# Seven products for two tiles of the last key group, and gated rows read back two steps later

## The chip, the cores and the metric

The kernel runs on one core of one Trainium2 chip. The metric is the device time of one execution in microseconds. Before the change it is 2479.84 us, the median of three runs (2478.89 to 2482.92).

## What is computed

An attention block without softmax is followed by a mixture of experts whose routing is a hash of the token number. Cut to what matters:

```python
# B, S, D, K = 8, 2496, 256, 64;  E, F = 8, 1024;  float32 throughout
scores = (1 / S) * z @ z.transpose(0, 2, 1)      # symmetric, S x S in each batch
x = u * (np.maximum(scores, 0) ** 2 @ v)         # B x S x D
x = x.reshape(B * S, D)
expert = token_ids * 2654435761 % E
for e in range(E):
    out[expert == e] = np.maximum(x[expert == e] @ w1[e], 0) @ w2[e]
```

## The kernel before

**Tiles and groups.** The 2496 tokens of a batch are 20 tiles of 128, the last of 64 rows. Four tiles make a group; groups are numbered g = 0 to 4, and batches b = 0 to 7. For each batch and each group of queries the kernel runs over the five groups of keys. Scores are symmetric, so a block of scores is computed once, with keys on the partitions; where the mirrored block is needed, it is turned by 32x32 transposes on VectorE. Some mirrors are turned in place of the tile, others go through one of three buffers named `stage` (L300) and are carried by DMAs of SyncE, `m<-stage` (L307). The attention phase fills about the first 1452 us, the MoE phase the rest.

**Key groups and their order.** `units` lists the groups of keys in the order in which a group of queries takes them. Its own group (the diagonal) comes last; the group of the last keys, k = 4, comes right before it when g is 1, 2 or 3. `mixed` says which key groups are computed by seven products of half-size blocks in place of eight (Winograd's form of Strassen's scheme): `product` issues one of them, and the table `PRODUCTS` gives the order, `[(1, 6), (5, 7), (2, 3), (4,)]`. A key group that is not mixed is taken tile by tile by `attend`, with two products of 512 columns for each tile, one for each half of the features; the last keys are one of these: three whole tiles, and the 64-row tile in `attend_last` at the start of the diagonal. All accumulate in four banks of PSUM, `acc`.

**Half-sums.** Four of the seven products need sums and differences of blocks of scores. `mix_a` makes them on GpSimd: three operations, L430 (two sums in one), L431 and L432, into one of two buffers `a_mix` (named `as`); a buffer comes free when its key group's products are done. `mix_a` is called at the start of each key group and ahead of the diagonal. Sums of the values, `v_mix` (named `vs`), are made on VectorE by `mix_v`.

**From the banks to the rows.** `post` (L462 to L468) adds the banks into `o_way`; `gate` (L475) transposes that into `x_q` on VectorE and puts three later steps on a list. After step i + 1, four DMAs of SyncE write the rows to DRAM (`x_way<-x_q`, L487). After step i + 3, SyncE reads them back as rows of tokens (`x_sb<-x_way`, L496). Five steps after that, `rows_by_u` copies the token numbers to the side of the rows on VectorE (L506) and multiplies the four tiles by u on GpSimd (L509). Then one tile after each step is scattered to `x_rows`, sorted by expert, with an indirect DMA on GpSimd (`place_x`, L749). One buffer `x_sb` and one `x_q` serve all groups.

**What sets the order.** The whole attention phase is written out by hand, in `tc.manual_schedule()`: after each step of products comes some work of ScalarE (squares of scores), some transposes, and `between`, which runs the steps of the list that are due and one scatter. Instructions of one engine run in the order in which they are issued here, and so do the DMAs of one queue.

Of the kernel before, what the change touches and what calls it, by code (L numbers as in the profile page):

```python
# [10 lines left out]
F32 = mybir.dt.float32  # L11
# [13 lines left out]
def kernel(  # L25
# [10 lines left out]
    nc = tc.nc  # L36
# [63 lines left out]
    zero = const.tile([P, W], F32)  # L100
    nc.gpsimd.memset(zero[:, 0:D], 0.0)
    nc.gpsimd.memset(zero[:, D:W].bitcast(I32), N)
    ident = const.tile([P, P], F32)
    make_identity(nc, ident[:])

# [2 lines left out]

    def group(g):
        return range(g * G, min(T, g * G + G))

    def tiles_io(dram, b, tiles, sb, store, eng, twice=False):

# [41 lines left out]
                    nc.scalar.dma_start(o[:, t], m)  # L157

    v_free = [vpool.tile([P, G, D], F32, name=f"v_{k}") for k in range(NG + 1)]
    v_mix = [vpool.tile([P, 4, G // 2, P], F32, name=f"vs_{k}") for k in range(NG - 1)]  # L160
    a_mix = [vpool.tile([P, 4, G * P], F32, name=f"as_{k}") for k in range(2)]
    o_way = vpool.tile([P, 4 * G * P // 2], F32, name="o_way")

    def load_v(b, g):
        v_sb[b, g] = v_free.pop(0)
# [4 lines left out]
    def mix_v(b, g):  # L170

        v = v_sb[b, g]
        (a11, a21), (a12, a22) = ([v[:, ts(k, G // 2), c::2] for c in range(2)] for k in range(2))
        s1, s2, s3, s4 = (v_mix[g][:, k] for k in range(4))
        nc.vector.tensor_add(s1, a21, a22)
        nc.vector.tensor_sub(s2, s1, a11)
        nc.vector.tensor_sub(s3, a11, a21)
        nc.vector.tensor_sub(s4, a12, s2)
# [5 lines left out]
    def turn_z(b, g):  # L184
        if g == 0:
            zT[b] = zpool.tile([P, T * P], F32, name="zT")
        if b:
            nc.vector.transpose(zT[b][:, ts(g, G * P)], zn[b][:, ts(g, G)].rearrange("p t j k -> p (t j k)"))
            return


        pairs = group(g) if g < NG else [T]
        ps = mm_ps.tile([P, G * P], F32, name="z_ps", tag="mm")
        for i, t in enumerate(pairs):
            nc.tensor.transpose(ps[:, ts(i, P)], zn[b][:, t:t + 2].rearrange("p t k -> p (t k)"), ident[:])
        i = 0 if g else 1
        n = len(pairs)
        copies = [nc.scalar.copy(zT[b][0:K, ds((g * G + i - 1) * P, (n - i) * P)], ps[0:K, i * P:n * P])]
        if g < NG:
            copies.append(nc.vector.tensor_copy(zT[b][K:P, ts(g, G * P)], ps[K:P, :]))  # L200

        for c, own, other in zip(copies, ("upper", "lower"), ("lower", "upper")):
            tc.declare_no_dep(c.ins, group=other, reason="other rows of zT")
            tc.add_to_no_dep_group(own, c.ins)
# [29 lines left out]

    def mixed(b, g, k):

        return k < NG - 1 and (b > 0 or g > 2)

    def skipped(b, g, t):

# [167 lines left out]
    def blocks(b, g, k):  # L408

        n = queries(g) // Q  # L410
        if k >= g:
            x = made[b, k, g] if k < g else made[b, g, k]
            return x[:].rearrange("p (k s) (h q) -> p k h s q", k=2, h=2)
        x = mirror[b, k, g][:].rearrange("p i r s q -> p (i r) (s q)")[:, 0:n]
        return x.rearrange("p (h n) (k y) -> p k h n y", h=2, k=2)

    def mix_a(most=2):

        for e in to_mix[:min(most, 2 - len(a_made))]:
            b, g, k = e  # L420
            turn_now((b, k, g))
            while any(x[0:2] == (b, g) and x[2] // G == k for x in to_square):
                square(1)
            tile = a_free.pop(0)
            n = queries(g)
            x = blocks(b, g, k)
            y = x.shape[3:]
            sums = [tile[:, m, 0:n].rearrange("p (n y) -> p n y", n=y[0]) for m in range(4)]
            t13 = tile[:, 0:2, 0:n].rearrange("p m (n y) -> p m n y", n=y[0])
            nc.gpsimd.tensor_sub(t13, x[:, :, 1], x[:, 0])  # L430
            nc.gpsimd.tensor_sub(sums[2], x[:, 1, 1], sums[0])  # L431
            nc.gpsimd.tensor_sub(sums[3], x[:, 1, 0], sums[2])  # L432
            a_made[e] = tile, sums
            to_mix.remove(e)

    def product(b, g, k, m):

        v, vs = v_sb[b, k], v_mix[k]
        n = queries(g) // Q // 2
        sums = a_made[b, g, k][1]  # L440
        for s in range(G // 2):
            if m in (1, 2, 4):
                w = v[:, s + (0 if m == 1 else 2), (1 if m == 4 else 0)::2]
            else:
                w = vs[:, {5: 0, 6: 1, 7: 2, 3: 3}[m], s]
            if m in (1, 2, 3):
                t = k * G + s + (0 if m == 1 else 2)
                x = squares(b, g, t)[:, ts(1 if m == 3 else 0, n)]
            else:
                x = sums[{5: 0, 7: 1, 6: 2, 4: 3}[m]]  # L450
                x = x[:, s].rearrange("p (n q) -> p n q", q=Q) if k >= g else x[:, :, ts(s, Q)]
            times((0, 1, 2, 3)[{1: 0, 6: 0, 5: 1, 7: 1, 2: 2, 3: 2, 4: 3}[m]], n * Q if m in (6, 7, 3) else 0, w, x)
# [17 lines left out]
    def gate(b, g, h):  # L470
        n = queries(g) // Q
        if h == 0:
            x_q[b, g] = qpool.tile([P, G * NQ, D // NQ], F32, name="x_q")
        x = x_q[b, g]
        nc.vector.transpose(x[:, 0:n, h::2], (o_way[:, ts(h, n * Q)] if any(mixed(b, g, k) for k in range(NG)) else acc[2 + h][:, 0:n * Q])  # L475
                            .rearrange("p (n q) -> p n q", q=Q))
        if h == 0:
            return

        xs = xpool.tile([P, G, W], F32, name="x_sb")  # L480
        o = x_way[groups.index((b, g)) % len(x_way)]

        ends = (b, g) == groups[-1]
        queues = [nc.sync, nc.scalar if ends else nc.sync]
        def rows_away():
            for a in range(NQ):
                queues[a % 2].dma_start(o[:].rearrange("n p d -> p n d")[:, 0:n, ts(a, D // NQ)], x[ts(a, Q), 0:n])  # L487
        if ends:
            rows_away()
        else:  # L490
            to_fetch.append((i + 1, rows_away))
        m = len(whole(g))
        def rows_of_x():

            w = o[:].rearrange("(i r) p d -> (r p) i d", r=NQ)
            queues[0].dma_start(xs[:, 0:m, 0:D], w[:, 0:m])  # L496
            if m < G:
                queues[0].dma_start(xs[0:R, m, 0:D], w[0:R, m])
            if (b, g) == groups[0]:
                load_u(b, g)  # L500
            to_fetch.append((i + 5, rows_by_u))
        def rows_by_u():
            for lo, n, rows in ((0, m, P), (m, len(group(g)) - m, R)):
                if n:
                    whose = token[0:rows, b, ds(g * G + lo, n)]
                    nc.vector.tensor_copy(xs[0:rows, lo:lo + n, D:W].bitcast(I32), whose.unsqueeze(2).to_broadcast([rows, n, W - D]))  # L506
            for k, t in enumerate(group(g)):
                y = xs[0:width(t), k, 0:D]
                (nc.vector if ends else nc.gpsimd).tensor_mul(y, y, u_sb[b, g][0:width(t), k, :])  # L509
                gated.append((b * T + t, xs[0:width(t), k, :]))  # L510
            if (b, g) == groups[-2]:
                while gated:
                    place_x()
            if not ends:
                to_fetch.append((i + 3, lambda: load_u(*groups[groups.index((b, g)) + 1])))
        to_fetch.append((max(i + 3, SORT + 2 + 14 * groups.index((b, g))), rows_of_x))

# [6 lines left out]
    extra = const.tile([1, 1], I32)  # L526
    slot_i = const.tile([P, C], I32)
    token = const.tile([P, B, T], I32)

    tok = const.tile([P, B, T, 2], I32)  # L530

    def clear_x(k):
        c = NW * BLK // P + k * -(-NT // CLEAR)
# [320 lines left out]
    for n, (b, g) in enumerate(groups):  # L854
# [10 lines left out]
        steps = []  # L865
        for x, k in enumerate(seq):
            last = k == g
            if mixed(b, g, k):
                banks = (0, 1, 2, 3) if x == 0 and g or last else (2, 1, 0, 3)
                part = [(lambda k=k, m=m: [product(b, g, k, e) for e in PRODUCTS[m]], m, 1 if m < 3 else 0.5) for m in banks]  # L870
            elif last:
                part = [(lambda t=[t for t in group(k) if t < TM], h=h: [attend(b, g, e, [h]) for e in t], 2 + h, 1.5)
                        for h in range(2)]
            else:
                part = [(lambda t=t: attend(b, g, t, range(2)), None, 1) for t in group(k) if t < TM]
            steps.append(part)
        t = 0
        for x, k in enumerate(seq):
# [18 lines left out]
            for y, (step, bank, weight) in enumerate(steps[x]):  # L897
                if k != g:
# [22 lines left out]
                            attend_last(b, g)  # L921
                    if b + 1 < B and (g, t) == (1, 9):
                        load_v(b + 1, NG - 1)
                    if (b, g) == (0, 2) and t in (4, 7, 10, 13):
                        mix_v(0, t // 3 - 1)
                if k == g and not ends and d:
                    scores(c, d, y * G, (y + 1) * G if y + 1 < len(steps[x]) else T)
                step()
# [483 lines left out]
```

## Time and profile before

| | before |
|---|---|
| median of three runs | 2479.84 us |
| the profiled execution | 2480.39 us |
| its span, first to last instruction | 2478.2 us |
| mean granted clock of TensorE | 0.996 |
| TensorE busy | 2448.0 us, 99% |
| VectorE busy | 1650.5 us, 67% |
| ScalarE busy | 740.5 us, 30% |
| GpSimd busy | 1322.2 us, 53% |

An engine's busy share is an average over both phases. In the page's names PE is the matmul unit, PEld its weight loads, DVE is VectorE, ACT ScalarE, POOL GpSimd, SP SyncE. The profile records each float32 matmul as two matmuls and two weight loads. In the rows of a timeline, instructions that follow each other without a gap and are alike stand as one row, with their count after an x.

### The profile page before, as it was taken

To read this page: it belongs to the slowest core of one execution; us is meant where nothing else is said; L and a number is where in the kernel's file an instruction comes from. 1 tells how busy PE (TensorE), PEld (TensorE's weight loads), DVE (VectorE), ACT (ScalarE), POOL (GpSimd) and SP (SyncE) were. 2 spreads that over 40 slices of the span, in tenths; PEclk is the share of its full clock that TensorE was granted. 3 is DMA by queue.
4 is the path that set the end of the run, shared out by engine and by line. 5 is a ranking of instruction groups with operands and counts; after the bars stand their busy time and mean duration, and the time that the engine had idled before them with its cause. 6 is when DMAs were issued, how large, how long until landed. Compare 5 with 4: busy or idle time off the path is not lost. (4 is left out here: it accounts for less than half of the span.)

```text
span 2478.2 us, 38152 instructions
## 1 busy us (share of the span) xinstructions
PE 2448.0 (99%) x12691; PEld 1963.8 (79%) x12691; DVE 1650.5 (67%) x3556; ACT 740.5 (30%) x1532; POOL 1322.2 (53%) x1078
## 2 busy tenths in 40 slices
PE   9999999999999999999999999999999999999998
PEld 4466777777777776776777769989998998998998
DVE  5887777787787786886787725556556556556534
ACT  5222324233232233234134102332232232323222
POOL 1357876776785876776777832333333333333314
PEclk9999999999999999999999999999999999999999
DMA  4364553454454535534534379769668767777751
GB/s 122 90 143 115 137 114 107 118 129 107 112 122 111 121 106 128 112 102 124 120 107 112 89 181 229 178 171 212 175 175 201 173 170 201 188 179 177 179 137 45
DMA packets 512966, 348.06 MB, mean 140 GB/s; under 512 B 289788, under 2 KB 475645, under 8 KB 512768
## 3 DMA queue, kind: packets, MB, share of 16 engines
q1 hardware_dynamic: 410512, 254.82, 42.9%
q10 hardware_dynamic: 86800, 48.57, 8.3%
q0 software_dynamic: 15456, 42.20, 5.1%
q8 instruction: 103, 1.69, 0.3%
q14 instruction: 95, 0.78, 0.1%
HBM read 231.19 MB, written 68.19 MB: 121 GB/s over the span
## 5 line engine op out<-in xcount | busy, mean ns | idle before, releaser
L268 ACT ACTIVATE a<-s_ps 128x512 f32<-128x512 f32 (+2 forms) x470 | 216.7, 547 | 930.4 <-PE s_ps L258 852.2
L403 PE MATMUL acc<-a,v 128*128 128x512 f32 (+4 forms) x1352 | 462.0, 507 | 0.0
L403 PE MATMUL acc<-as,vs 128*128 128x256 f32 (+1 forms) x1776 | 422.0, 378 | 13.6 <-POOL as L431 9.7
L403 PEld LDWEIGHTS acc<-a,v 128*128 128x128 f32 (+1 forms) x1352 | 243.5, 196 | 183.3 <-issue 151.1
L403 PEld LDWEIGHTS acc<-as,vs 128*128 128x128 f32 x1776 | 336.8, 191 | 64.7 <-POOL as L431 13.7
L1278 POOL DMA_INDIRECT out_dram<-as,ids x120 | 123.2, 1027 | 469.4 <-DVE as L1177 441.2
L296 DVE STREAM_TRANSPOSE m<-a 32x512 f32<-32x512 f32 (+1 forms) x512 | 350.6, 685 | 8.7 <-ACT a L274 0.8
L324 DVE STREAM_TRANSPOSE a<-a 32x128 f32<-32x128 f32 (+2 forms) x1360 | 286.6, 241 | 13.2 <-ACT a L274 2.3
L274 ACT ACTIVATE a<-a 128x512 f32<-128x512 f32 (+1 forms) x480 | 238.3, 591 | 22.7 <-DMA m<-stage 22.5
L1050 PE MATMUL h_ps<-v,as 128*128 128x256 f32 x904 | 223.7, 380 | 0.0
L300 DVE STREAM_TRANSPOSE stage<-a 128x512 f32<-128x512 f32 x192 | 131.1, 696 | 127.4 <-DMA m<-stage 126.4
L258 PE MATMUL s_ps<-zT 64*128 64x512 f32 (+1 forms) x960 | 212.5, 558 | 1.3 <-ACT a L274 0.9
L430 POOL TENSOR_TENSOR as<-a 128x1024 f32<-128x1024 f32 x71 | 169.1, 2382 | 74.2 <-ACT a L274 39.7
L749 POOL DMA_INDIRECT x_rows<-x_sb,slot_i x160 | 158.2, 989 | 91.1 <-issue 28.9
L430 POOL TENSOR_TENSOR as<-m 128x1024 f32<-128x1024 f32 (+1 forms) x77 | 173.6, 2254 | 41.0 <-DMA m<-stage 29.8
L509 POOL TENSOR_TENSOR x_sb<-x_sb,u_sb 128x256 f32<-128x256 f32 (+1 forms) x156 | 109.6, 735 | 158.1 <-DMA x_sb<-x_way 135.7
L1050 PEld LDWEIGHTS h_ps<-v,as 128*128 128x128 f32 x904 | 171.9, 190 | 23.4 <-DVE v L1029 0.4
L403 PE MATMUL acc<-m,v 128*128 128x256 f32 (+2 forms) x664 | 177.2, 392 | 1.7 <-issue 1.5
L258 PEld LDWEIGHTS s_ps<-zT 64*128 64x128 f32 x960 | 98.9, 187 | 93.0 <-issue 60.3
L1066 DVE TENSOR_TENSOR hT<-stage,h_ps 128x512 f32<-128x512 f32 x111 | 76.2, 687 | 134.2 <-PE h_ps L1050 130.1
L403 PEld LDWEIGHTS acc<-m,v 128*128 128x128 f32 x664 | 126.9, 197 | 47.4 <-issue 38.6
L403 PE MATMUL acc<-as,v 128*128 128x256 f32 (+1 forms) x592 | 149.4, 375 | 0.0
(220 smaller groups left out, 3829.2 us busy)
## 6 DMA issues: line engine op xcount, KB each, us to landing
m<-in_moe_w_dram SPq DMA_DIRECT2D x200, 256.0 KB
m<-in_moe_w_dram SPq DMA_DIRECT2D x50, 1024.0 KB
m<-stage SPq DMA_DIRECT2D x576, 64.0 KB
x_way<-x_q SPq DMA_DIRECT2D x128, 128.0 KB
u_sb<-in_u_dram ACTq DMA_DIRECT2D x32, 512.0 KB
x_sb<-x_way SPq DMA_DIRECT2D x32, 512.0 KB
v<-x_rows SPq DMA_DIRECT2D x128, 128.0 KB
zn<-in_moe_w_dram SPq DMA_DIRECT2D x64, 256.0 KB
```

Of the source, the lines that this page charges most:

```text
L258: nc.tensor.matmul(ps[:, lo:n], zT[b][h, ts(t, P)], zT[b][h, ds(g * G * P + lo, n - lo)], start=True, stop=True)
L268: nc.scalar.activation(a, ps[:, lo:n], AF.Relu)
L274: nc.scalar.activation(a, a, AF.Square, scale=1.0 / S)
L296: nc.vector.transpose(o, x[ts(r, Q), 0:m * G, ts(c, Q)].rearrange("p (i s) q -> p i s q", s=G))
L300: nc.vector.transpose(stage[:].rearrange("p (n q) -> p n q", q=Q), x[:, :, ts(c, Q)])
L324: return n * Q, lambda: nc.vector.transpose(out, in_)
L403: nc.tensor.matmul(acc[k][:, ds(at, n)], weights, x, start=k not in begun, stop=True, skip_group_check=True)
L430: nc.gpsimd.tensor_sub(t13, x[:, :, 1], x[:, 0])
L509: (nc.vector if ends else nc.gpsimd).tensor_mul(y, y, u_sb[b, g][0:width(t), k, :])
L749: st = nc.gpsimd.indirect_dma_start(out=x_dram[:, :], out_offset=bass.IndirectOffsetOnAxis(ap=slot_i[0:width(c % T), c:c + 1], axis=0), in ...
L1050: nc.tensor.matmul(ps[:, ts(i, W)], terms[k][0][:, ts(2 * d + i, P)], terms[k][1], start=first and i == 0, stop=True, skip_group_check=True)
L1278: st = nc.gpsimd.indirect_dma_start(out=out[:], out_offset=bass.IndirectOffsetOnAxis(ap=rows, axis=0), in_=o, in_offset=None, bounds_check ...
```

## The change

**Which groups are mixed.** Where products are mixed at all, the last keys are now mixed for the query groups 1, 2 and 3. That holds in seven batches for three groups and in the first batch for group 3. Of the last keys' three whole tiles, tile 18 is still taken plainly, as the first step; tiles 16 and 17 are one block of two halves, one tile each, and their seven products are the second and third steps: (2, 3, 1, 6) and (5, 7, 4). `half(k)` gives the tiles in a half: 2, or 1 for the last keys. For this there is a fifth buffer of value sums and four VectorE operations per batch. To make room for it, the token table `tok` and the identity `ident` now lie in `o_way`, which they use before the first `post` writes it.

**When rows come back.** The read-back of the gated rows is put on the list for i + 5 in place of i + 3; the multiply still follows five steps after it. The copy of the token numbers moves from ahead of the multiply to ahead of the read-back.

```diff
+    def half(k):
+        return G // 2 if k < NG - 1 else 1
...
-    v_mix = [vpool.tile([P, 4, G // 2, P], F32, name=f"vs_{k}") for k in range(NG - 1)]
+    v_mix = [vpool.tile([P, 4, half(k), P], F32, name=f"vs_{k}") for k in range(NG)]
...
+    tok = o_way[:, 0:B * T * 2].bitcast(I32).rearrange("p (b t two) -> p b t two", b=B, two=2)
+    ident = o_way[:, ds(B * T * 2, P)]
+    make_identity(nc, ident)
...
     def mixed(b, g, k):
-        return k < NG - 1 and (b > 0 or g > 2)
+        return (b > 0 or g > 2) and (k < NG - 1 or 0 < g < NG - 1)
...
-            x = made[b, k, g] if k < g else made[b, g, k]
-            return x[:].rearrange("p (k s) (h q) -> p k h s q", k=2, h=2)
+            x = made[b, g, k][:, 0:2 * half(k), 0:queries(g)]
+            return x.rearrange("p (k s) (h q) -> p k h s q", k=2, h=2)
...
         def rows_of_x():
+            for lo, n, rows in ((0, m, P), (m, len(group(g)) - m, R)):
+                if n:
+                    whose = token[0:rows, b, ds(g * G + lo, n)]
+                    nc.vector.tensor_copy(xs[0:rows, lo:lo + n, D:W].bitcast(I32), whose.unsqueeze(2).to_broadcast([rows, n, W - D]))
             w = o[:].rearrange("(i r) p d -> (r p) i d", r=NQ)
             queues[0].dma_start(xs[:, 0:m, 0:D], w[:, 0:m])
...
             to_fetch.append((i + 5, rows_by_u))
         def rows_by_u():
-            for lo, n, rows in ((0, m, P), (m, len(group(g)) - m, R)):
-                if n:
-                    whose = token[0:rows, b, ds(g * G + lo, n)]
-                    nc.vector.tensor_copy(xs[0:rows, lo:lo + n, D:W].bitcast(I32), whose.unsqueeze(2).to_broadcast([rows, n, W - D]))
...
-        to_fetch.append((max(i + 3, SORT + 2 + 14 * groups.index((b, g))), rows_of_x))
+        to_fetch.append((max(i + 5, SORT + 2 + 14 * groups.index((b, g))), rows_of_x))
...
-            if mixed(b, g, k):
+            if mixed(b, g, k) and k == NG - 1 and not last:
+                part = [(lambda: attend(b, g, TM - 1, range(2)), None, 1)]
+                part.extend((lambda k=k, m=m: [product(b, g, k, e) for e in m], None, 1) for m in ((2, 3, 1, 6), (5, 7, 4)))
+            elif mixed(b, g, k):
...
-                    if (b, g) == (0, 2) and t in (4, 7, 10, 13):
-                        mix_v(0, t // 3 - 1)
+                    if (b, g) == (0, 2) and t in (1, 4, 7, 10, 13):
+                        mix_v(0, (t // 3 - 1) % NG)
+                    if b and (g, t) == (0, 9):
+                        mix_v(b, NG - 1)
```

GpSimd in a second group (g = 1) of a later batch, from the fourth key group's half-sums to the diagonal's; `as` is a half-sum buffer, `a` a block of scores, L430 to L432 and after them L436 to L438 are the three operations of `mix_a`. Before:

```order
L430 TENSOR_TENSOR as_107<-a 128x1024
L431 TENSOR_TENSOR as_107<-a,as_107 128x512
L432 TENSOR_TENSOR as_107<-a,as_107 128x512
L509 TENSOR_TENSOR x_sb<-x_sb,u_sb 128x256 x4
L749 DMA x_rows<-x_sb,slot_i 20480x272 x2
L430 TENSOR_TENSOR as_108<-a 128x1024
L431 TENSOR_TENSOR as_108<-a,as_108 128x512
L432 TENSOR_TENSOR as_108<-a,as_108 128x512
L749 DMA x_rows<-x_sb,slot_i 20480x272 x2
```

And now:

```order
L436 TENSOR_TENSOR as_104<-a 128x1024
L437 TENSOR_TENSOR as_104<-a,as_104 128x512
L438 TENSOR_TENSOR as_104<-a,as_104 128x512
L436 TENSOR_TENSOR as_103<-a 128x2x256
L437 TENSOR_TENSOR as_103<-a,as_103 128x256
L438 TENSOR_TENSOR as_103<-a,as_103 128x256
L515 TENSOR_TENSOR x_sb<-x_sb,u_sb 128x256 x4
L753 DMA x_rows<-x_sb,slot_i 20480x272 x4
L436 TENSOR_TENSOR as_104<-a 128x1024
L437 TENSOR_TENSOR as_104<-a,as_104 128x512
L438 TENSOR_TENSOR as_104<-a,as_104 128x512
```

The last keys' half-sums stand between the fourth key group's and the multiply, and the diagonal's half-sums stand behind four scatters in place of two.

TensorE at the end of the same group, the last keys and the start of the diagonal; `v` are values, `vs` their sums, `s_ps` scores of the next group. Before:

```order
L403 MATMUL acc<-a,v_101 128x512 x8
L258 MATMUL s_ps<-zT 128x512 x4
L403 MATMUL acc<-a,v_98 128x256 x2
L403 MATMUL acc<-as_108,vs_104 128x256 x2
L258 MATMUL s_ps<-zT 128x512 x4
```

And now:

```order
L409 MATMUL acc<-a,v_96 128x512 x2
L409 MATMUL acc<-a,v_96 128x256
L409 MATMUL acc<-a,vs_102 128x256
L409 MATMUL acc<-a,v_96 128x256
L409 MATMUL acc<-as_104,vs_102 128x256 x3
L409 MATMUL acc<-as_104,v_96 128x256
L409 MATMUL acc<-a,v_96 128x512 x2
L264 MATMUL s_ps<-zT 128x512 x4
L409 MATMUL acc<-a,v_93 128x256 x2
L409 MATMUL acc<-as_103,vs_99 128x256 x2
```

Four of the eight products of 512 columns (six of three whole tiles, two of the 64-row tile) became seven of 256, and four of those read half-sums of GpSimd.

VectorE in the first group (g = 0) of a later batch, around the copy of the token numbers of the group before; `stage` are carried mirrors, `m` mirrors turned in place. Before:

```order
L296 STREAM_TRANSPOSE m_192<-a 32x4x128
L300 STREAM_TRANSPOSE stage<-a 128x512 x4
L506 COPY x_sb<-token 128x4x16
L300 STREAM_TRANSPOSE stage<-a 128x512 x5
L462 COPY o_way<-acc 128x256
```

And now:

```order
L302 STREAM_TRANSPOSE m_191<-a 32x4x128 x3
L504 COPY x_sb<-token 128x4x16
L302 STREAM_TRANSPOSE m_191<-a 32x4x128
L306 STREAM_TRANSPOSE stage<-a 128x512 x3
L181 TENSOR_TENSOR vs_102<-v_97 128x128
L182 TENSOR_TENSOR vs_102<-vs_102,v_97 128x128
L183 TENSOR_TENSOR vs_102<-v_97 128x128
L184 TENSOR_TENSOR vs_102<-v_97,vs_102 128x128
L306 STREAM_TRANSPOSE stage<-a 128x512 x5
L468 COPY o_way<-acc 128x256
```

The copy stood among the transposes of the carried mirrors and now stands ahead of them; the four sums of the last keys' values have come in among them.

## Rows read from the trace of the kernel before

**Rows 1.** The page, section 1: busy time of each engine, share, instructions.
```profile
PE 2448.0 (99%) x12691; PEld 1963.8 (79%) x12691; DVE 1650.5 (67%) x3556; ACT 740.5 (30%) x1532; POOL 1322.2 (53%) x1078
```
**Rows 2.** TensorE's waits: line waited for, us in total, times, longest us.
```profile
PE acc L403 <- POOL as L431: 9.7, 10, 4.9
```
**Rows 3.** Timeline, TensorE: start, us, instruction, [idle before it and what ended it].
```profile
214.55 6.18 PE L403 MATMUL acc<-a,v 128*128 128x512 f32 x16
...
619.32 1.03 PE L403 MATMUL acc<-a,v 128*128 128x256 f32 x4
620.18 1.03 PE L403 MATMUL acc<-a,vs 128*128 128x256 f32 x4
...
635.05 1.13 PE L403 MATMUL acc<-as,vs 128*128 128x256 f32 x4 [0.53 <-POOL as L431]
```
**Rows 4.** Timeline, GpSimd, first and second group of the fourth batch.
```profile
587.65 1.01 POOL L749 DMA_INDIRECT x_rows<-x_sb,slot_i  x1 [3.60 <-DVE x_sb L506]
...
592.45 2.38 POOL L430 TENSOR_TENSOR as<-a 128x1024 f32<-128x1024 f32 x1
...
626.04 2.77 POOL L509 TENSOR_TENSOR x_sb<-x_sb,u_sb 128x256 f32<-128x256 f32 x4 [7.79 <-DMA x_sb<-x_way]
628.96 1.01 POOL L749 DMA_INDIRECT x_rows<-x_sb,slot_i  x1 [0.15 <-POOL x_sb L509]
...
631.27 2.38 POOL L430 TENSOR_TENSOR as<-a 128x1024 f32<-128x1024 f32 x1
633.73 1.27 POOL L431 TENSOR_TENSOR as<-a,as 128x512 f32<-128x512 f32 x1
```
**Rows 5.** Timeline, SyncE's DMA issues, second group of the fourth batch.
```profile
585.69 29.88 SPq L307 DMA_DIRECT2D m<-stage  x44
615.68 3.30 SPq L487 DMA_DIRECT2D x_way<-x_q  x4
619.08 2.55 SPq L307 DMA_DIRECT2D m<-stage  x4
621.95 0.38 SPq L496 DMA_DIRECT2D x_sb<-x_way  x1
```
**Rows 6.** Groups by line and form: count | busy us, mean ns | idle before.
```profile
L403 PEld LDWEIGHTS acc<-as,vs 128*128 128x128 f32 x1776 | 336.8, 191 | 64.7 <-POOL as L431 13.7 <-issue 11.7 <-POOL as L430 4.6
```
**Rows 7.** Timeline, GpSimd and TensorE, diagonals of other second groups.
```profile
455.17 1.26 POOL L431 TENSOR_TENSOR as<-a,as 128x512 f32<-128x512 f32 x1
...
457.93 1.03 PE L403 MATMUL acc<-as,vs 128*128 128x256 f32 x4
...
811.67 1.13 PE L403 MATMUL acc<-as,vs 128*128 128x256 f32 x4 [0.57 <-POOL as L431]
...
1165.48 1.13 PE L403 MATMUL acc<-as,vs 128*128 128x256 f32 x4 [1.20 <-POOL as L431]
...
1343.54 1.13 PE L403 MATMUL acc<-as,vs 128*128 128x256 f32 x4 [0.97 <-POOL as L431]
```
**Rows 8.** Timeline, GpSimd and TensorE, first group of the second batch.
```profile
234.65 1.01 POOL L749 DMA_INDIRECT x_rows<-x_sb,slot_i  x1 [6.74 <-DVE x_sb L506]
...
240.70 2.07 PE L403 MATMUL acc<-as,vs 128*128 128x256 f32 x4 [4.90 <-POOL as L431]
```
**Rows 9.** Timeline, GpSimd and TensorE, end of attention, first MoE product.
```profile
1436.58 2.10 POOL L430 TENSOR_TENSOR as<-m 128x896 f32<-128x896 f32 x1
...
1438.73 3.35 PE L403 MATMUL acc<-as,vs 128*128 128x224 f32 x8 [3.45 <-POOL as L430]
...
1453.81 15.70 PE L995 MATMUL h_ps<-v,m 128*128 128x512 f32 x32 [2.52 <-DVE v L843]
```
**Rows 10.** Windows: us, then PE, PEld, DVE, ACT, POOL busy, PEclk, DMA, GB/s.
```profile
240.80:246.40 5.60, 5.60 (x12) 2.26 (x12) 1.73 (x3) 1.09 (x2) 5.13 (x4) 0.50 0.56 148
1438.80:1444.40 5.60, 5.60 (x15) 5.04 (x16) 0.00 (x0) 0.00 (x0) 2.21 (x2) 0.50 0.49 97
1454.80:1458.10 3.30, 3.30 (x5) 1.32 (x4) 0.00 (x0) 0.60 (x1) 0.00 (x0) 0.50 0.45 87
1165.50:1172.00 6.50, 6.50 (x30) 4.07 (x31) 2.58 (x5) 3.03 (x6) 5.94 (x5) 1.00 0.57 144
```

More of the change, by code (lines that the diff above doesn't have):

```diff
@@ L102 @@
     nc.gpsimd.memset(zero[:, D:W].bitcast(I32), N)
-    ident = const.tile([P, P], F32)
-    make_identity(nc, ident[:])
     def width(t):
@@ L172, in mix_v @@
         v = v_sb[b, g]
-        (a11, a21), (a12, a22) = ([v[:, ts(k, G // 2), c::2] for c in range(2)] for k in range(2))
+        (a11, a21), (a12, a22) = ([v[:, ts(k, half(g)), c::2] for c in range(2)] for k in range(2))
         s1, s2, s3, s4 = (v_mix[g][:, k] for k in range(4))
@@ L194, in turn_z @@
         for i, t in enumerate(pairs):
-            nc.tensor.transpose(ps[:, ts(i, P)], zn[b][:, t:t + 2].rearrange("p t k -> p (t k)"), ident[:])
+            nc.tensor.transpose(ps[:, ts(i, P)], zn[b][:, t:t + 2].rearrange("p t k -> p (t k)"), ident)
         i = 0 if g else 1
@@ L424, in mix_a @@
             tile = a_free.pop(0)
-            n = queries(g)
             x = blocks(b, g, k)
             y = x.shape[3:]
+            n = y[0] * y[1]
             sums = [tile[:, m, 0:n].rearrange("p (n y) -> p n y", n=y[0]) for m in range(4)]
@@ L440, in product @@
         sums = a_made[b, g, k][1]
-        for s in range(G // 2):
+        for s in range(half(k)):
             if m in (1, 2, 4):
-                w = v[:, s + (0 if m == 1 else 2), (1 if m == 4 else 0)::2]
+                w = v[:, s + (0 if m == 1 else half(k)), (1 if m == 4 else 0)::2]
             else:
@@ L446, in product @@
             if m in (1, 2, 3):
-                t = k * G + s + (0 if m == 1 else 2)
+                t = k * G + s + (0 if m == 1 else half(k))
                 x = squares(b, g, t)[:, ts(1 if m == 3 else 0, n)]
@@ L528 @@
     token = const.tile([P, B, T], I32)
-    tok = const.tile([P, B, T, 2], I32)
     def clear_x(k):
```

## The prediction

> **What bounds the kernel now.** The page's first section comes first: TensorE is busy in 2448.0 of 2478.2 us [rows 1], so the time is the length of TensorE's instructions and the few gaps between them. An edit counts if it shortens that queue, or opens or closes a gap. The list of TensorE's waits comes second: ten waits for the second half-sum of scores that GpSimd makes for a diagonal group (line 431) hold 9.7 us, the longest 4.9 [rows 2]. The reader should see in these rows that the bank products already lean on GpSimd, and with how little room. The third view shows by how little: in the second group of the fourth batch TensorE stood 0.53 us before the diagonal's first product on half-sums, at 635.05 [rows 3]. GpSimd was late since its order there is multiply by u, two scatters, diagonal mix, and the multiply, free after 7.79 us of idling, waited for the rows to come back from DRAM until 626.04; the scatters began at 628.96, the mix at 631.27, and its second part began at 633.73 and took 1.27 [rows 4]. SyncE says why the rows came then: 44 sends of mirror stages without a gap from 585.69, then the four writes of x_way, four more sends, then the read-back at 621.95 [rows 5]. That chain is paced by VectorE's transposes into three stage buffers, not by TensorE.
>
> **Columns saved.** The last keys' three whole tiles cost two products of 512 columns for each half, each recorded as two matmuls. The 16 records from 214.55 are twelve of those and four of 256 columns, 6.18 us in all; four of 256 alone are recorded with 1.03 us, so one of 512 takes (6.18 - 1.03) / 12 = 0.43 us, and as the next four follow 0.86 us later (619.32 to 620.18), one of 256 takes 0.215 [rows 3]. Two of the tiles are 8 x 0.43 = 3.44 us; seven products on their halves are 14 x 0.215 = 3.01. A saving of 0.43 us in each of 22 groups (three in seven batches, one in the first) gives **-9.4 us**, all on the path.
>
> Each of the 14 records has a weight load of its own, where there were 8. In this kernel 1776 such loads take 191 ns each [rows 6], and the records above still follow each other in 215 ns, so the loads lie beside the matmuls. The Trainium skill ("TensorE: Matmul & The Clock Gate", Part 3, "The mechanism") says that a weight load overlaps matmuls in flight only when its row group differs, and here all have all 128 rows. By that rule 14 x (0.215 + 0.19) = 5.7 us would replace 8 x (0.43 + 0.19) = 5.0, and the change would lose 0.7 x 22 = 15 us; the trace does not agree, since 256-column records of one row group stand 0.215 apart, not 0.41.
>
> **The new sums.** GpSimd makes the last keys' half-sums at half size. No row has that size; the full ones take 2.38 and 1.27 us [rows 4], and the third, of the second's size, as much, so half is 2.5 and the whole size, the upper bound, 4.9. I take 2.8, nearer the half with some start cost. They can begin when products free the second buffer (about 619.3 in the stretch above) and end at 622, within the 7.79 us idle; TensorE wants them only behind one plain tile and four records. Cost 0, and up to 2 us a group if the idle were absent. VectorE's four value sums (four operations of 128x128 a batch) go beside 67% busy VectorE: 0. Token numbers and the identity sharing the output buffer: 0, since both are read before it is written.
>
> **Scatters ahead of the diagonal's mix.** One scatter is issued each step. The read moves two steps later in the program, but SyncE issues it as soon as what stands ahead of it in its queue is through; in the second groups that queue's 44 sends and the four writes are the same, so the rows land at the same time. The multiply still waits for them and GpSimd's order becomes: last keys' sums, multiply, **four** scatters, diagonal mix. Behind the waiting multiply stand the mix and TensorE's products. Four scatters before a mix took 592.45 - 587.65 = 4.80 us, two took 631.27 - 628.96 = 2.31 [rows 4]: the mix is 2.5 later. TensorE also arrives 0.4 sooner by the columns and 0.3 sooner by the gaps of the first groups, closed below. So the margin of each second group shrinks by 3.2. Four of the six such groups waited already (0.53 [rows 3], 0.57, 1.20 and 0.97 [rows 7], 3.3 together), and each waits 3.2 more: 3.7 to 4.4. In the other two the mix was ready early: its second part ended at 455.17 + 1.26 = 456.4 where the product began at 457.93 [rows 7]; less that margin of 1.5 each waits 1.7. Together 4 x 3.2 + 2 x 1.7 = **+16.2 us**. If the rows landed earlier this goes to zero (a rival); if by two steps later, up to 3 us a group more.
>
> In the third and fourth groups the order is the same, but 12 stage sends stand ahead of the writes, where the second groups have 16 to 24, so rows return earlier than TensorE's need by an estimated 2 to 4 us. I take +3 for all of them and the two odd groups of the first two batches, between 0 and 26.
>
> **Gaps that close.** In the first group of the second batch a scatter waited 6.74 us for VectorE's token copy, which stood in a run of stage transposes, and TensorE waited 4.90 us for the mix behind it [rows 8]. With the copy issued ahead of the read that goes. The other five waits (9.7 - 4.9 - 3.3 = 1.5 us) are in first groups with the same order and go too. In the last group the mix of the fourth key group moves ahead of the multiply and scatters, so the wait of 3.45 us at 1438.73 goes; but the last eight scatters now come behind its three parts, some 4 us later (the first part alone takes 2.10), and the MoE part's first product, at 1453.81 after a gap of 2.52, waits for rows that they write [rows 9].
>
> **The clock.** After idles of 4.90, 3.45 and 2.52 us [rows 8, 9] TensorE's granted clock was 0.50 (1.2 GHz) for 5.6, 5.6 and 3.3 us of the stretches shown; after the wait of 1.20 us [rows 7] it stayed at 1.00 [rows 10]. Half the time is lost: 2.8, 2.8 and 1.65 us. So closing the first two gives 4.90 + 2.8 = **-7.7** and 3.45 + 2.8 = 6.3, of which the later start of the MoE part takes back 2 to 6: **-3.5**. The four waits of 3.7 to 4.4 us lie between 2.52 and 4.90; I price each at the mean of 1.65 and 2.8, 2.3: **+9.2**, bounds 0 and 11. The two of 1.7 us lie nearer 1.20: 0.
>
> **The sum.** -9.4 - 7.7 - 1.5 - 3.5 + 16.2 + 9.2 + 3 = +6.3 us. The profiled execution took 2480.4 (2478.2 of span and 2.2 around it), so 2486.7; the median is 0.55 lower: **2486**.
>
> **Rivals.** (a) *No new wait, the other side.* If the last sends ahead of x_way finish some 4 us sooner once VectorE's token copies leave the transposes' way, the rows land early, the existing second-group waits (3.3) vanish and no new ones come: -9.4 - 7.7 - 1.5 - 3.3 - 3.5 + 3 = -22.4, so 2457.5. It decides from a multiply that begins 3.2 us or more earlier against TensorE than 626.04. For it: GpSimd idles 7.79 us just there [rows 4]. Against it: the sends run gapless from 585.69 [rows 5] and a token copy is one short operation. (b) *The waits come, the clock stays.* Without its 9.2 us the sum is -2.9: 2477. For it: only three such idles are on record. (c) *The third and fourth groups wait as well*, 12 of them by 2 us, with the 24 in place of 2 of the 3: 2508. For it: the same order on GpSimd; against it: fewer sends ahead. (d) *Loads not hidden*, the rule above: +15 for -9.4, 2511. *That the change does not do what it says* has no room: the products replace the tiles in TensorE's order in 22 groups.
>
> **Chances.** Forecast 46% (2478 to 2495), (a) 21%, (b) 19%, (c) 11%, (d) 3%. A measurement of this kernel can tell some 0.2%, 5 us, from no change. (a) and a fifth of (b) are faster: 25%. The rest of (b) and the lowest tenth of the forecast are within: 20%. The rest is slower: 55%. The range leaves out the lower part of (a), about 9%, and the upper half of (c) with (d), 9%: 2457 to 2507. The forecast's own is 2478 to 2495.
>
> **What would show it.** Right: TensorE's waits on line 437 (431 before) gather at the diagonals of the second groups, 3.5 to 4.5 us each, with a clock of 0.50 behind them; the scatters run by fours ahead of the diagonal mix; multiplies still idle for the rows; the gaps of 4.90 and 3.45 are gone; last keys' records stand 0.215 apart. Wrong: a multiply that begins early enough, or waits that appear at the last keys' products instead, which would put the price on the new sums.

## The result and the profile after

The changed kernel takes 2509.3 us in the median (2505.2 to 2514.3, six runs) against 2480.3 before (2478.0 to 2482.9): 1.0115 times as long, with a 95% interval of 1.0105 to 1.0125. It is slower by some 29 us, as forecast in sign, but by five times the +6 of the sum, and 2 us past the upper end of the range. The profiled execution took 2513.8 us, 4.5 above the median; the sums below are made against its own span.

The page's first lines, and the list of TensorE's waits (engine, what waited, line waited for: us in total, times, longest). L436 to L438 are the three parts of `mix_a`, L468 to L474 `post`, L504 the token copy, L506 the read-back, L515 the multiply, L753 the scatter:

```profile
span 2512.1 us, 38566 instructions
PE 2457.3 (98%) x12823; PEld 1994.1 (79%) x12823; DVE 1690.7 (67%) x3588; ACT 741.8 (30%) x1532; POOL 1381.7 (55%) x1144
PE acc L409 <- POOL as L437: 26.2, 10, 4.1
PE acc L409 <- POOL as L436: 3.6, 2, 3.1
PE acc L409 <- DVE o_way L469: 3.5, 1, 3.5
PE h_ps L1059 <- DVE vs L847: 2.1, 1, 2.1
```

The 9.7 us of [rows 2] have become 26.2, again in ten waits, and TensorE is busy 9.3 us longer [rows 1] although its queue has fewer columns: the clock was at half more often, as the next table shows.

To find where the 33.9 us of span went, I cut TensorE's timeline at the start of each group's diagonal, and each piece into waits, time lost to half clock (half of every stretch at a granted clock of 0.50, as far as TensorE was not waiting in it), and the rest. Numbers in us, after minus before; a second group has g = 1, a fourth g = 3:

| where | waits | half clock | forecast |
|---|---|---|---|
| six diagonals of second groups | +15.9 | +12.4 | +16.2 and +9.2 |
| diagonals of fourth groups (four of them) | +7.1 | +1.7 | +3 with all others |
| first batch, its last group (g = 4) | +3.5 | +1.5 | 0 |
| first batch, its fourth group | -0.7 | 0 | 0 |
| second batch, first group | -0.8 | +0.1 | -7.7 |
| five other first groups | -1.6 | 0 | -1.5 |
| small new waits for `post` (first and last groups) | +2.8 | 0 | 0 |
| fourth key group's half-sums in the last group | -3.5 | -2.9 | -6.3 |
| start of the MoE part | +2.1 | +1.7 | +2.8 |
| the rest, mostly columns | -6.6 | | -9.4 |

(With 1.3 us at the program's start, which varies as much between the runs below, the waits, the half clock and the rest sum to the 33.9 within 0.1.)

The second group of the fourth batch, GpSimd and then TensorE, is what was forecast:

```profile
639.49 2.78 POOL L515 TENSOR_TENSOR x_sb<-x_sb,u_sb 128x256 f32<-128x256 f32 x4 [4.92 <-DMA x_sb<-x_way]
642.42 1.01 POOL L753 DMA_INDIRECT x_rows<-x_sb,slot_i  x1 [0.15 <-POOL x_sb L515]
...
646.31 0.98 POOL L753 DMA_INDIRECT x_rows<-x_sb,slot_i  x1 [0.30 <-issue]
647.31 2.36 POOL L436 TENSOR_TENSOR as<-a 128x1024 f32<-128x1024 f32 x1
649.74 1.26 POOL L437 TENSOR_TENSOR as<-a,as 128x512 f32<-128x512 f32 x1
...
651.06 1.13 PE L409 MATMUL acc<-as,vs 128*128 128x256 f32 x4 [3.48 <-POOL as L437]
```

From the multiply's start to the diagonal's half-sums it is 7.8 us, where it was 5.2 [rows 4]: two scatters more. GpSimd idled 4.92 us for the rows where it had idled 7.79; the last keys' half-sums fitted in there, and TensorE had no wait at the last keys. Behind this 3.48 us wait the clock was at half, and behind that of 3.85 us at 1195.54 for twice as long (columns as in [rows 10]):

```profile
652.60:655.80 3.20, 3.20 (x9) 0.96 (x6) 1.10 (x3) 1.25 (x3) 3.12 (x2) 0.50 0.12 28
1195.60:1202.00 6.40, 6.40 (x14) 2.95 (x15) 1.47 (x3) 1.72 (x4) 6.08 (x4) 0.50 0.13 29
```

In the fourth group of the third batch the read-back came later against TensorE. SyncE's queue, GpSimd and TensorE before, then the same after, with TensorE's wait:

```profile
505.21 2.40 SPq L487 DMA_DIRECT2D x_way<-x_q  x4
510.18 0.38 SPq L496 DMA_DIRECT2D x_sb<-x_way  x1
...
522.41 1.27 POOL L431 TENSOR_TENSOR as<-a,as 128x512 f32<-128x512 f32 x1
...
526.82 1.46 PE L403 MATMUL acc<-as,vs 128*128 128x256 f32 x6
```
```profile
516.30 2.49 SPq L493 DMA_DIRECT2D x_way<-x_q  x4
518.89 3.40 SPq L313 DMA_DIRECT2D m<-stage  x4
522.54 0.40 SPq L506 DMA_DIRECT2D x_sb<-x_way  x1
...
527.69 2.78 POOL L515 TENSOR_TENSOR x_sb<-x_sb,u_sb 128x256 f32<-128x256 f32 x4 [3.78 <-DMA x_sb<-x_way]
...
535.50 2.37 POOL L436 TENSOR_TENSOR as<-a 128x1024 f32<-128x1024 f32 x1
...
539.27 4.11 PE L409 MATMUL acc<-as,vs 128*128 128x256 f32 x10 [2.40 <-POOL as L437]
```

Two steps later in the program, four stage sends (3.40 us) now lie between the writes and the read-back. The read-back comes 6.2 us after the writes began, not 5.0. Before, the half-sum that the product needs was ready 3.1 us ahead of it (522.41 + 1.27 against 526.82); now it is 2.4 us late. Of these 5.5 us, 2.6 are the two scatters more between the multiply and the half-sums, and 2.9 the later multiply. From the third batch on, such new sends between writes and read-back stand in the third and the sixth batch alone; the waits in the fourth groups of the fourth and the seventh batch (0.7 and 1.1 us) come without them.

In the first two batches three things are new. VectorE stood idle at two token copies, waiting for the scatters of the group ahead:

```profile
193.94 0.50 DVE L504 COPY x_sb<-token 128x64 int32<-128x64 int32 x1 [2.36 <-DMA x_rows<-x_sb,slot_i]
277.72 0.49 DVE L504 COPY x_sb<-token 128x64 int32<-128x64 int32 x1 [3.77 <-DMA x_rows<-x_sb,slot_i]
```

After the first of these, VectorE's value sums ran while GpSimd made half-sums. TensorE waited for the banks to be added. VectorE, GpSimd, TensorE:

```profile
202.70 3.05 DVE L181 TENSOR_TENSOR vs<-v 128x256 f32<-128x256 f32 x1
205.85 1.30 DVE L182 TENSOR_TENSOR vs<-vs,v 128x256 f32<-128x256 f32 x1
207.08 1.49 DVE L183 TENSOR_TENSOR vs<-v 128x256 f32<-128x256 f32 x1
208.49 2.56 DVE L184 TENSOR_TENSOR vs<-v,vs 128x256 f32<-128x256 f32 x1
...
203.07 2.38 POOL L436 TENSOR_TENSOR as<-a 128x1024 f32<-128x1024 f32 x1
205.53 1.34 POOL L437 TENSOR_TENSOR as<-a,as 128x512 f32<-128x512 f32 x1
206.95 1.33 POOL L438 TENSOR_TENSOR as<-a,as 128x512 f32<-128x512 f32 x1
208.25 2.52 POOL L436 TENSOR_TENSOR as<-a 128x1024 f32<-128x1024 f32 x1
...
212.60 2.07 PE L409 MATMUL acc<-a,v 128*128 128x256 f32 x4 [3.52 <-DVE o_way L469]
```

Each sum ends 0.3 us after one of GpSimd's operations. And in the next group the rows of the group ahead were read back at 259.52, behind twenty sends, so the multiply and the half-sums behind it were late in place of the closed gap:

```profile
244.68 14.61 SPq L313 DMA_DIRECT2D m<-stage  x20
259.52 0.41 SPq L506 DMA_DIRECT2D x_sb<-x_way  x1
...
263.38 2.77 POOL L515 TENSOR_TENSOR x_sb<-x_sb,u_sb 128x256 f32<-128x256 f32 x4 [5.18 <-DMA x_sb<-x_way]
...
271.04 3.78 PE L409 MATMUL acc<-as,vs 128*128 128x256 f32 x8 [3.11 <-POOL as L436]
```

### The profile page after: what moved, and what is told of

Same layout as the page of the kernel before. It is cut to its first block, busy times and chain, and to the rows that moved or that the text cites. A ratio compares the mean times of both kernels' runs of the same rounds, so it can differ in the third digit from the quotient of the medians.

```text
span 2512.1 us, 38566 instructions
## 1 busy us (share of the span) xinstructions
PE 2457.3 (98%) x12823; PEld 1994.1 (79%) x12823; DVE 1690.7 (67%) x3588; ACT 741.8 (30%) x1532; POOL 1381.7 (55%) x1144
## 5 line engine op out<-in xcount | busy, mean ns | idle before, releaser
L409 PE MATMUL acc<-as,vs 128*128 128x256 f32 (+1 forms) x1908 | 459.9, 381 | 31.7 <-POOL as L437 26.2
L409 PEld LDWEIGHTS acc<-as,vs 128*128 128x128 f32 x1908 | 364.3, 193 | 90.9 <-POOL as L437 30.4
L409 PE MATMUL acc<-a,v 128*128 128x256 f32 (+4 forms) x1264 | 412.6, 488 | 3.5 <-DVE o_way L469 3.5
L409 PEld LDWEIGHTS acc<-a,v 128*128 128x128 f32 (+1 forms) x1264 | 226.8, 197 | 148.8 <-issue 109.6
L436 POOL TENSOR_TENSOR as<-a 128x1024 f32<-128x1024 f32 (+1 forms) x93 | 196.4, 2111 | 105.1 <-PE acc L409 63.0
L264 PE MATMUL s_ps<-zT 64*128 64x512 f32 (+1 forms) x960 | 218.1, 571 | 0.6 <-DVE zT L194 0.5
L753 POOL DMA_INDIRECT x_rows<-x_sb,slot_i x160 | 158.6, 991 | 74.0 <-issue 30.5
L436 POOL TENSOR_TENSOR as<-m 128x1024 f32<-128x1024 f32 (+1 forms) x77 | 173.2, 2249 | 47.4 <-DMA m<-stage 34.2
L409 PE MATMUL acc<-as,v 128*128 128x256 f32 (+1 forms) x636 | 162.9, 376 | 2.1 <-DVE o_way L474 1.5
L515 POOL TENSOR_TENSOR x_sb<-x_sb,u_sb 128x256 f32<-128x256 f32 (+1 forms) x156 | 110.9, 743 | 83.8 <-DMA x_sb<-x_way 83.5
```

The source lines that it names most:

```text
L264: nc.tensor.matmul(ps[:, lo:n], zT[b][h, ts(t, P)], zT[b][h, ds(g * G * P + lo, n - lo)], start=True, stop=True)
L409: nc.tensor.matmul(acc[k][:, ds(at, n)], weights, x, start=k not in begun, stop=True, skip_group_check=True)
L753: st = nc.gpsimd.indirect_dma_start(out=x_dram[:, :], out_offset=bass.IndirectOffsetOnAxis(ap=slot_i[0:width(c % T), c:c + 1], axis=0), in ...
```

## Experiments

Theory A: the loss is made by the place of the multiply, which waits for rows, and of the scatters in GpSimd's order. Rival B: a later read-back in SyncE's queue costs by itself. Rival C: the products cost what they save. A2 is on the first batch: the token copy holds VectorE.

**1. Read-back nine steps after the gate.**

```diff
-        to_fetch.append((max(i + 5, SORT + 2 + 14 * groups.index((b, g))), rows_of_x))
+        to_fetch.append((max(i + 9, SORT + 2 + 14 * groups.index((b, g))), rows_of_x))
```

> The changed kernel with the read-back of rows nine steps after the gate in place of five: on GpSimd the diagonal's half-sums then stand ahead of the multiply and of all four scatters. Theory A (GpSimd's order: the diagonal's half-sums stand behind a multiply that waits for rows, and behind four scatters): the waits of 2.4 to 4.1 us at the diagonals of second and fourth groups (26 us in all) go, with the 13 us of half clock behind them; about 2470 us. Theory B (the read-back comes too late in SyncE's queue, behind more stage sends): later is worse, over 2510 us. Theory C (products of 256 columns with their weight loads cost more than the two plain tiles): no change, about 2509 us.

Measured: 2504.7 us, 1.0086 (1.0066 to 1.0107). The diagonal waits of second and fourth groups for GpSimd were gone, all of them, as A said; the time was 35 us off. TensorE now waited for ScalarE, 26 us in 11 waits, mostly in first groups. GpSimd, ScalarE's queue and ScalarE, TensorE in the fourth batch's first group:

```profile
602.52 2.76 POOL L515 TENSOR_TENSOR x_sb<-x_sb,u_sb 128x256 f32<-128x256 f32 x4 [8.05 <-DMA x_sb<-x_way]
...
605.31 0.35 ACTq L128 DMA_DIRECT2D u_sb<-in_u_dram  x1
605.75 2.06 ACT L274 ACTIVATE a<-s_ps 128x512 f32<-128x512 f32 x4 [36.39 <-DMA m<-stage]
...
606.40 4.05 PE L264 MATMUL s_ps<-zT 64*128 64x512 f32 x8 [3.96 <-ACT a L274]
```

ScalarE's load of the next u overwrites the one buffer of u. It went out at 605.31, 0.03 us after the multiply had ended (602.52 + 2.76), and the scores of the next group stood behind it in ScalarE's queue. It is the same at the ten longest of the eleven waits. (Most of the 36.39 us ScalarE has no work; before the change it idles 30 us there.) The multiply has a second customer, and a later multiply keeps it waiting.

**2. Seven steps.** The same line with `i + 7`.

> The changed kernel with the read-back seven steps after the gate: on GpSimd the diagonal's half-sums stand behind the multiply and two scatters, as they did before the change, and the last keys' half-sums ahead of the multiply. Theory A: each diagonal wait of second and fourth groups is 2.5 us shorter, so those of second groups shrink from 3.1 to 4.1 to about 0.6 to 1.6 and fourth groups to under 0.4, and the clock stays up: about 2479 us. Theory B: over 2509 us. Theory C: about 2509 us.

Measured: 2493.7 us, 1.0039 (1.0026 to 1.0052), 16 us below five steps, but 15 above what was expected. Second groups' waits fell to 1.0, 0.3, 0.2 and three times nothing, those of fourth groups to 1.3 us and less. In four first groups waits of 3.0 to 4.3 us came up, since there the half-sums now stood behind the multiply, and the wait at the start of the MoE part grew from 2.5 to 5.9 us. One of the four:

```profile
600.16 2.77 POOL L515 TENSOR_TENSOR x_sb<-x_sb,u_sb 128x256 f32<-128x256 f32 x4 [14.97 <-DMA x_sb<-x_way]
603.08 1.01 POOL L753 DMA_INDIRECT x_rows<-x_sb,slot_i  x1 [0.15 <-POOL x_sb L515]
604.12 2.35 POOL L436 TENSOR_TENSOR as<-a 128x1024 f32<-128x1024 f32 x1
...
607.87 2.08 PE L409 MATMUL acc<-as,vs 128*128 128x256 f32 x4 [4.30 <-POOL as L437]
```

So B is wrong as the account of the loss (both later read-backs are faster) and A is right on the mechanism, but no single number of steps that was tried suits all groups.

**3. The rows' part alone**, on the kernel before: the token copy moved to `rows_of_x`, and

```diff
-        to_fetch.append((max(i + 3, SORT + 2 + 14 * groups.index((b, g))), rows_of_x))
+        to_fetch.append((max(i + 5, SORT + 2 + 14 * groups.index((b, g))), rows_of_x))
```

> The kernel before with the change's treatment of rows alone (read-back five steps after the gate, token numbers copied ahead of it), without the seven products for the last keys. GpSimd's order then has the diagonal's half-sums ahead of the multiply. Theory A: the diagonal waits of before (3.3 us) and of first groups (1.5 us) go and the last group's 6.9 us, of which 4 come back at the MoE start; the first two batches lose up to 5 us as in the changed kernel: 2473 to 2478 us. Theory B: the later read-back alone costs the 20 us and more that the change costs, about 2500 us. Theory C: as A.

Measured: 2480.9 us, 0.9992 (0.9982 to 1.0002). Without products nothing waits at the diagonals, and the last group gains 6.6; the first batch and the next group lose 6.2. It is some 3 us above what was expected.

**4. The token copy alone**, on the kernel before: the copy moved to `rows_of_x`, three steps kept.

> The kernel before with the token numbers copied ahead of the read-back and nothing else. The gap of 4.9 us in the first group of the second batch is behind that copy. If closing it gives what was forecast, 2480 - 7.7 - 1.5 = about 2471 us. If VectorE's value sums collide with GpSimd's half-sums at the end of the first batch, and the rows then return behind the stage sends in any case, as in the changed kernel, the 4.9 us reappear at the next products and 5 us are added: 2480 to 2485 us.

Measured: 2488.8 us, 1.0023 (1.0012 to 1.0035), slower, and beyond the dearer of the two cases. VectorE stood still at a copy for 5.10 us in the first batch:

```profile
198.37 0.50 DVE L498 COPY x_sb<-token 128x64 int32<-128x64 int32 x1 [5.10 <-DMA x_rows<-x_sb,slot_i]
```

In this part of the change the forecast had its second gain (-7.7), and alone it is a loss.

**5. The changed kernel with the first batch's copies back ahead of the multiply** (`whose_x` is the token copy).

```diff
+        def whose_x():
...
         def rows_of_x():
+            if b:
+                whose_x()
...
         def rows_by_u():
+            if not b:
+                whose_x()
```

> The changed kernel with the token copies of the first batch alone put back ahead of the multiply. In the changed kernel VectorE stood idle at two such copies (2.4 and 3.8 us), since they overwrite the one row buffer before the scatters of the group ahead have left it. Theory A2 (the copy holds VectorE, its value sums then run beside GpSimd's half-sums and are held by them, and the banks of the first batch's last group are added late): the wait of 3.5 us at 212 us and its 1.7 to 3.4 us of half clock go, the 4.9 us gap in the next group comes back in place of 3.1 and 0.8: about 2504 us. If the first batch's loss has to do with the seven products there: no change, 2509 us.

Measured: 2507.7 us (2504.3 to 2512.3), 1.0111 (1.0095 to 1.0128). Some 2504 was expected; in time it can't be told from the changed kernel. In the trace the wait of 3.5 us is gone; VectorE's sums there lie ahead of the scatters and of GpSimd's half-sums, and take 0.42 us each:

```profile
200.78 0.42 DVE L181 TENSOR_TENSOR vs<-v 128x256 f32<-128x256 f32 x1
201.31 0.43 DVE L182 TENSOR_TENSOR vs<-vs,v 128x256 f32<-128x256 f32 x1
...
204.04 1.01 POOL L758 DMA_INDIRECT x_rows<-x_sb,slot_i  x1 [5.22 <-DVE o_way L469]
```

In this trace, counted from the first scores, TensorE reaches the second batch's second diagonal 7.8 us earlier than in the changed kernel's. The medians don't show it: the executions of both kernels spread over 8 to 9 us.

**6 to 8. A number of steps for each group**, then with two ways to treat the first batch's copy: two steps after the read-back (7), and as in 5 (8).

```diff
-        to_fetch.append((max(i + 5, SORT + 2 + 14 * groups.index((b, g))), rows_of_x))
+        to_fetch.append((max(i + (7, 5, 9, 9, 5)[g], SORT + 2 + 14 * groups.index((b, g))), rows_of_x))
```

> The changed kernel with the read-back 7, 5, 9, 9, 5 steps after the gates of groups 0 to 4, so that in no group with a late row the diagonal's half-sums stand behind the multiply and four scatters. Theory A (the place of multiply and scatters in GpSimd's order makes the waits, each group having its own best place): diagonal waits of second and fourth groups are under 1 us as in the two runs with seven and with nine steps, those that these two had in first groups (3 to 4.3 us) don't come, 2468 to 2473 us. Theory B (any later read-back costs): over 2500 us.

Measured: 2468.6 us, 0.9946 (0.9929 to 0.9962), as expected. Waits for L437 are 4.5 us in all, the longest 1.1; no half clock behind a diagonal's wait.

> The same delays, and the first batch's token copies two steps after the read-back in place of ahead of it. Theory A2: VectorE no longer idles for the scatters, the 3.5 us wait at 212 us goes; some of it comes back in the next group, where rows return behind the stage sends: 2463 to 2470 us, 2 to 5 us below the same delays with the early copy.

Measured: 2469.1 us, 0.9947 (0.9930 to 0.9963). The 3.5 us wait went, but the time did not, a miss by 2 us or more. In the two traces, counted from the first scores, run 7 is 3.0 us ahead of run 6 at the second batch's second diagonal and 1.6 us in the last batch; what takes this back isn't shown.

> The same delays, and the first batch's token copies where they were before the change, ahead of the multiply. Theory A2: as the run before it, with the 4.9 us gap of the second batch's first group in place of other waits there: 2463 to 2470 us.

Measured: 2463.4 us (2463.4 to 2465.0), 0.9929 (0.9912 to 0.9946), as expected. **This version beats both kernels**, the one before by 18 us. Its waits for L437 (the longest, 3.0 us, is what is left of the 4.90 us gap in the second batch's first group), and one at a second group's diagonal:

```profile
PE acc L409 <- POOL as L437: 6.5, 5, 3.0
```
```profile
624.82 1.01 POOL L758 DMA_INDIRECT x_rows<-x_sb,slot_i  x1 [0.16 <-POOL x_sb L520]
626.14 0.98 POOL L758 DMA_INDIRECT x_rows<-x_sb,slot_i  x1 [0.30 <-issue]
627.13 2.37 POOL L436 TENSOR_TENSOR as<-a 128x1024 f32<-128x1024 f32 x1
...
630.90 1.13 PE L409 MATMUL acc<-as,vs 128*128 128x256 f32 x4 [1.63 <-POOL as L437]
```

With two scatters ahead of the half-sums, not four, it is half of the 3.48 us.

**9. The rows' part with five steps and the first batch's late copy, without products.** The edits of 3 and 5 on the kernel before.

> The kernel before, read-back five steps after the gate, token numbers copied ahead of it except in the first batch, no products for the last keys. With the last keys plain, the diagonal's half-sums stand ahead of the multiply in every group already. Against the run with delays and the first batch's late copy this differs by the products alone. Theory A with the columns as forecast (0.43 us in each of 22 groups): 9 us above that run, 2472 to 2474 us. If the products' gain is eaten by their weight loads or by GpSimd's extra half-sums: no difference, 2463 to 2465 us.

Measured: 2475.4 us, 0.9969 (0.9958 to 0.9979), 1 us above what was expected. The version with products (run 8) is 12.0 us faster. The two differ in the number of steps as well, so the time alone doesn't settle C; TensorE's busy time does, without and with products:

```profile
PE 2446.9 (99%) x12691; PEld 1964.8 (79%) x12691; DVE 1651.1 (67%) x3556; ACT 740.3 (30%) x1532; POOL 1319.6 (53%) x1078
```
```profile
PE 2436.8 (99%) x12823; PEld 1984.9 (81%) x12823; DVE 1675.3 (68%) x3588; ACT 740.5 (30%) x1532; POOL 1378.8 (56%) x1144
```

It is 10.1 us shorter with 132 records more. Of these, 1.6 us are less time at half clock, so the products themselves save some 8.5 us, and C is wrong.

**10. The products alone**, rows as before the change.

> The kernel before with the seven products for the last keys alone; rows are read back three steps after the gate and token numbers copied ahead of the multiply, as before. In second and fourth groups GpSimd then has the multiply, waiting for rows, and two scatters ahead of the last keys' half-sums, and two more scatters ahead of the diagonal's. Theory A: waits move to the last keys' products, 4 to 6 us each in six second groups and 0 to 3 in the fourth, with half clock behind them, and the first batch is as before: 2510 to 2535 us. Theory B (the later read-back makes the change's loss): about 2470 us.

Measured: 2536.8 us, 1.0224 (1.0206 to 1.0241), 2 us past the upper end of what was expected.

```profile
PE acc L409 <- POOL as L437: 49.9, 29, 5.3
```

Waits of 2.2 to 5.3 us at the last keys' products in second groups, and of up to 2.4 us in third and fourth groups. So the two later steps are not what costs: the products with the rows as before lose 55 us, with the later rows the whole change loses 29.

## Why the prediction was wrong

- **Columns saved: right.** -9.4 forecast; some -8.5 between runs 9 and 8. The table's rest is -6.6 and holds other small differences too: a group without a wait in either trace is 0.41 us shorter, for 0.43 forecast. The rival on hidden loads (d) is out.
- **The new sums: right.** No wait at the last keys in the changed kernel; they ran in GpSimd's idle time. "Cost 0" held with five steps; with three (run 10) the longest waits of all, up to 5.3 us, stood there.
- **Four scatters ahead of the diagonal's mix: right.** 15.9 us of waits for 16.2, each within 2 us of its own forecast; runs 1, 2 and 6 take most or all of them away by moving multiply and scatters alone. In part the sum is luck: the third batch's wait is 1.8 us over its forecast, since rows came later there too, and others are under theirs.
- **The clock behind them: mis-sized.** 12.4 for 9.2, past its upper bound of 11. The price of one was nearly right, 2.5 on average for 2.3; the forecast counted four, and five had half clock behind them. The fifth is the third batch's, where it had 1.7 us of waiting and 3.50 came.
- **"I take +3" for third and fourth groups: mis-sized.** 8.8 in the fourth groups, none in the third. Two things went into it. The estimate that rows return 2 to 4 us early was too high: before the change the half-sums were ready only 1.4 to 1.6 us ahead of TensorE in the fourth groups of the fourth, sixth and seventh batches, and two scatters more take 2.6. And in the third and sixth batches I did not count the sends that came between the writes and the read-back when the read-back was moved two steps past them in SyncE's queue; the two waits there (2.40 and 2.86 us) are the longest.
- **"With the copy issued ahead of the read that goes" (-7.7): the step that failed most.** The two groups around it took 5.0 us longer (4.3 of them are in the table's two rows), 12.7 us off. "Token numbers ... 0, since both are read before it is written" looked at the output buffer and not at the row buffer that the copy writes: there is one, and VectorE stopped until the scatters had left it. Its four sums, which then ran beside GpSimd's, took 8.4 us, where they take 1.7 in run 5. Run 4 shows the copy alone to be a loss; runs 5 and 8 put the first batch's copies back, and the 3.5 us wait is gone. The gap closed, and the next late thing, rows behind twenty stage sends, took 3.11 of its 4.90 us, with the clock no better.
- **The end of attention: right.** -6.4 and +3.8 for -6.3 and +2.8.

Of the rivals, (c) had the time, 2508, but not the mechanism: it asked for 12 waits, and four came. (a) did not happen: in the second groups the multiply began between 0.5 us earlier and 2.4 us later against TensorE than before, where (a) asked for 3.2 earlier. (b) did not either: the clock fell to 0.50 behind five of the six waits.

What stays open: why run 7 is not faster than run 6, and why the executions of the changed kernel spread over 9 us. Their mean granted clock differs: 0.990 to 0.991 in the three longest, 0.993 to 0.994 in the three shortest; by my estimate 0.003 of 2510 us is 7.5 us, most of the spread. Which waits came and went isn't shown, as there is one trace of it, of one of the longest.

## What to carry to other kernels

A gain on the bounding engine is worth what the queues behind it can bear: list, for each engine and DMA queue, what a moved step now stands in front of, and count the instructions between its two neighbours, not only those ahead of the first. A copy that is issued "early, where nothing waits for it" still waits for the buffer that it writes, and holds everything behind it on its engine. Where one delay serves groups of different shape, price each group apart: here the kernel with the same products is 55 us slower with three steps, 29 with five, and 18 faster with a number for each group and the first batch's copies left where they were.

## What the runs showed of the hardware

VectorE's sums of two SBUF tensors were held by GpSimd's. In the changed kernel all 71 value sums that took over 0.8 us ended 0.15 to 0.29 us after a GpSimd sum or product ended; 74 that met none took 0.28 to 0.43 us, and 15 that met one for a shorter time 0.28 to 0.70 us. The 256-column sums of a bank and `o_way` (one operand in PSUM) took 0.39 to 0.42 us whether GpSimd was at work or not. The Trainium skill ("GPSIMD Engine Reference", "8. Key points") says that GpSimd shares its SBUF interfaces with VectorE and contends with instructions that have two SBUF inputs; the traces agree, and show VectorE's sum lasting until GpSimd's operation has ended: 3.05 us at 202.70 for 0.42 us of work, 3.21 us at the longest.
